# A four-layer sliding-attention kernel: a new set of planner costs and instruction orders, constant tables as planned tasks, weight scales computed in groups

## The chip, the core and the metric

The kernel runs on one core of a Trainium2 chip. A core has five engines that each work through their own instruction stream in order and wait for each other through semaphores: TensorE (PE, matmuls; its weight loads are listed as PEld), VectorE (DVE), ScalarE (ACT), GpSimd (POOL) and SyncE (SP, which here only starts DMA transfers). SBUF is the memory that the engines work in, PSUM the eight accumulator banks that PE writes and DVE and ACT read. The metric is the device time of one execution in microseconds, the median of several runs. All times below are in us unless marked ns.

## What is computed

Four layers A, B, A, B on `x` of 2048 positions by 512, each `x = x + layer(layernorm(x))`, with 32 heads of 16. Layer A is a dilated local attention: each position sees eight positions, 0, 2, ..., 14 back. Layer B is a block attention: each position sees itself and the 255 before it.

```
def _A_ref(x, wqkv, wo):            # W, dil = 8, 2
    q, k, v = split(x @ wqkv)
    idx = pos[:, None] - off[None, :]            # off = 0, 2, ..., 14
    logits = einsum("bhsd,bhswd->bhsw", q, k[idx]) * scale
    attn = softmax(where(idx >= 0, logits, -1e9))
    return einsum("bhsw,bhswd->bhsd", attn, v[idx]) @ wo

def _B_ref(x, wqkv, wo):            # W = 256
    q, k, v = split(x @ wqkv)
    scores = einsum("bhqd,bhkd->bhqk", q, k) * scale
    mask = (i - j >= 0) & (i - j < W)
    return einsum("bhqk,bhkd->bhqd", softmax(where(mask, scores, -1e9)), v) @ wo

x = x + A(layernorm(x));  x = x + B(layernorm(x))       # and both once more
```

## The kernel before

The sequence is cut into eight chunks of 256 positions. The work is done chunk by chunk in pairs of layers: `layer_a(0, c)` and `layer_b(1, c)` for c = 0 to 7, then `layer_a(2, c)` and `layer_b(3, c)`. In the tables these sixteen pairs are called A0, B0 to A15, B15. All matmuls of the projections are done with a high and a low half of both operands in 16 bits: `xh`, `xl` of the normalized input, `wA0h`, `wA0l` and so on of the weights (s = 0, 1, 2 for q, k, v and 3 for the output).

Before any projection the weights are prepared by `prep` (L765), for A and then for B. For each of the four parts: two DMA loads of 512 KB (into the buffers `stk`, which hold layer B's stacked operands later, or into `stage` for the output weights); the sum of squares per partition (L807 on ACT, L809 on DVE); two transposes on PE that put it in one row; on DVE a chain of a reduce and five operations on one number (L823 to L829, called a scale chain below); a matmul with ones that spreads the two factors to all partitions (L832); a copy to `psc` (L836); and then a split in two halves each, the high one on ACT (L860), the low one on DVE (L864). The first B loads use the `stk` buffers of A's weights and so wait for A's splits.

`norm` (L875) takes a chunk's statistics on DVE (L888 to L894), the power -0.5 on POOL (L897, operand `mhalf`), one more small operation on DVE (L900), normalizes on ACT (L915), transposes on PE (L919) and splits into `xh` (L924, ACT) and `xl` (L925, DVE). `proj_t` (L944 to L946) and `proj_n` (L964 to L967) are the projections.

`layer_a` (L1018) forms products of q with shifted k, four tiles `pr` per group and four groups (L1077, on DVE, some on POOL), which PE reduces over the head's 16 elements with the selector `sel` (L1085). Softmax follows (L1108 to L1120), its last operation a high/low split. PE spreads the weights over the head's elements with `selt` (L1154); DVE multiplies with v (L1167, the weighing, tiles `pw`, three buffers); the sum over the eight positions is three operations on POOL (L1174 to L1176) or one reduce on DVE (L1172). `finish` (L978) splits the result (L987, L989), projects it and adds it to x (L995).

`layer_b` (L1183) writes its q and k halves to DRAM and reads them back stacked (L1208, L1219). A first set of scores (L1262, L1265) only serves the row maximum: DVE overwrites the masked part (L1284) and reduces (L1280). In the first chunk of a layer there is nothing before it, and one custom operation does mask and maximum (L1276). The maximum goes to the operand by a DMA (L1317, L1323), and a second set of scores (L1356, L1358) goes through the exponential on ACT (L1362) and a mask on POOL (L1371) to the matmul with v (L1388). The sums come back through DRAM, and the division is a multiplication on DVE or POOL (L1462).

What sets the order: every piece above is a task, handed to `Plan.add` with its engine, a duration in us, what it reads and writes, and sometimes another engine (`alt`). The table `ORDER` holds one number for each task, its place in its engine's queue; a negative number -1 - n means place n on the other engine. `Plan.order` plays the tasks through with the durations, the `LAG` between engines, the cost `LEAVE` of a change in the kind of matmul, and DMA sizes; each engine takes its tasks in the order of places, and the play decides in which order the program is written out and which PSUM bank and buffer a task gets. On the chip every engine then follows its stream. The tables `maskt`, `sel`, `selt` and the ones in `v` are built on POOL before the first task. 330 matmuls without use (L1497, 110 tasks of three, table "W") keep PE active where it would idle.

## Time and profile before

| | |
|---|---|
| median of 3 runs | 1451.04 (1451.01 to 1454.21) |
| profiled execution | 1455.91 |
| its span, first to last instruction | 1454.0 |
| mean granted TensorE clock over the span | 0.969 |
| instructions | 35256 |
| DMA | 97.40 MB, mean 67 GB/s |

The profile is of one execution. Its own time is 4.9 above the median of the three runs, and 1.9 of it lies outside the span. A row of a timeline gives start, length, engine, line, operation, output and input, count, and in brackets the idle time of the engine before it with what ended it. A row by group gives the count, then busy time and mean ns of one, then idle time. In windows, busy time of each engine in each stretch is followed by the granted clock of TensorE, 1.00 being full speed.

### The profile page before, as it was taken

What the parts mean: (1) busy time and instruction counts of PE and PEld (TensorE: products, weight loads), DVE (VectorE), ACT (ScalarE), POOL (GpSimd) and SP (SyncE); (2) the same over time, 40 slices, a digit from 0 to 9 for tenths busy, and PEclk for the clock granted to TensorE, in tenths of its full rate; (3) what the DMA queues carried; (4) which work ended last, traced back from release to release, by engine and by line L of the source; (5) the groups of instructions that cost most, each with busy time, mean ns of one, the idle gap of its engine ahead of it and who ended that gap; (6) DMA issues with size and microseconds to landing.
All of it is one profiled execution on the core that took longest, in us unless ns stands there. A gap on an engine that the chain in (4) does not pass through costs nothing.

```text
span 1454.0 us, 35256 instructions
## 1 busy us (share of the span) xinstructions
PE 1351.0 (93%) x14058; PEld 796.1 (55%) x14058; DVE 1197.2 (82%) x2313; ACT 735.1 (51%) x1051; POOL 656.0 (45%) x752
## 2 busy tenths in 40 slices
PE   7698999989899999999989998998999999998998
PEld 4374655637465463745537364654647456474654
DVE  7958699797978979798887869798797988979693
ACT  6431335554555555555554434555454555545654
POOL 2504145372724627263471716446272553717342
PEclk9899899999999999999999998999999999999999
DMA  7030122212221221212122222222222122122221
GB/s 260 16 86 24 42 61 66 72 44 89 49 68 50 71 85 37 96 38 71 57 51 90 54 90 51 68 59 53 82 55 92 36 76 64 51 83 54 71 70 44
DMA packets 89221, 97.40 MB, mean 67 GB/s; under 512 B 34016, under 2 KB 60128, under 8 KB 89056
## 3 DMA queue, kind: packets, MB, share of 16 engines
q1 hardware_dynamic: 88800, 94.89, 23.2%
q8 instruction: 110, 1.80, 0.5%
q14 instruction: 55, 0.45, 0.1%
q10 hardware_dynamic: 256, 0.26, 0.1%
HBM read 50.33 MB, written 35.09 MB: 59 GB/s over the span
## 4 chain that ended last, share of the span: by engine, by line
PE 53%; DVE 22%; POOL 10%; issue 5%; DMA 5%; ACT 4%; SPq 1%; DVEq 0%; POOLq 0%; ACTq 0%
PE banks L944 9%; PE banks L945 8%; PE banks L946 8%; PE banks L1388 6%; DVE m L1280 4%; PE banks L1085 4%; POOL pw L1174 3%; DVE pw L1167 3%; DVE banks L1284 3%; PE banks L1356 3%; PE banks L966 3%; PE banks L964 2%; PE banks L1262 2%; PE banks L967 2%; PE banks L919 2%
## 5 line engine op out<-in xcount | busy, mean ns | idle before, releaser
L1362 ACT ACTIVATE p<-banks,sclB 128x768 f32<-128x768 f32 x480 | 419.8, 900 | 269.0 <-PE banks L1358 202.8
L1371 POOL TENSOR_SCALAR_AFFINE_SELECT p<-p 128x1024 f32<-128x1024 f32 x240 | 263.8, 1105 | 414.7 <-ACT p L1362 381.0
L1280 DVE TENSOR_REDUCE m<-banks 128x2 f32<-128x512 f32 x448 | 298.2, 685 | 5.0
L1284 DVE COPY_PREDICATED banks<-maskt,banks 128x256 f32<-128x256 int16 x448 | 180.6, 422 | 68.5 <-PE banks L1265 58.3
L1388 PE MATMUL banks<-p,v 128*32 128x128 f32 (+1 forms) x3840 | 197.0, 331 | 5.5 <-POOL p L1371 4.3
L1077 DVE TENSOR_TENSOR pr<-kv,q 128x512 f32<-128x512 f32 x239 | 162.9, 733 | 40.4 <-PE banks L1085 14.1
L1388 PEld LDWEIGHTS banks<-p,v 128*32 128x32 f32 x3840 | 106.0, 109 | 100.1 <-issue 38.0
L1167 DVE TENSOR_TENSOR pw<-banks,kv 128x1024 f32<-128x1024 f32 x128 | 152.6, 1213 | 2.9 <-POOL o L1176 2.0
L1356 PE MATMUL banks<-stk,stk 64*128 64x256 f16 x960 | 134.9, 282 | 21.5 <-DVE m L1280 6.6
L1174 POOL TENSOR_TENSOR pw<-pw 128x512 f32<-128x512 f32 x101 | 128.3, 1270 | 15.1 <-DVE pw L1167 14.5
L1262 PE MATMUL banks<-stk,stk 48*128 48x128 f16 (+1 forms) x896 | 112.8, 253 | 20.5 <-DVE m L1280 9.8
L1265 PE MATMUL banks<-stk,stk 48*128 48x256 f16 (+1 forms) x1024 | 127.1, 249 | 4.6 <-DVE pw L1167 1.9
L1356 PEld LDWEIGHTS <-stk 64*128 64x128 f16 x960 | 56.2, 95 | 104.7 <-issue 100.1
L1358 PE MATMUL banks<-stk,stk 64*128 64x128 f16 x960 | 108.0, 221 | 0.0
L1262 PEld LDWEIGHTS <-stk 48*128 48x128 f16 x896 | 50.3, 94 | 102.9 <-issue 98.7
L915 ACT ACTIVATE xn<-x,rs 128x512 f32<-128x512 f32 x64 | 52.0, 812 | 77.6 <-DVE rs L900 62.5
L1175 POOL TENSOR_TENSOR pw<-pw 128x256 f32<-128x256 f32 x101 | 74.8, 741 | 7.9
L1085 PE MATMUL banks<-pr,sel 128*32 128x512 f32 x512 | 70.4, 602 | 2.6 <-DVE pr L1077 2.5
L944 PE MATMUL banks<-xh,wB1h 128*128 128x256 f16 x256 | 70.6, 276 | 0.0
L944 PE MATMUL banks<-xh,wA2h 128*128 128x256 f16 x256 | 70.4, 275 | 0.1
L945 PE MATMUL banks<-xl,wA0h 128*128 128x256 f16 x256 | 69.8, 273 | 0.7 <-DVE xl L925 0.7
L944 PE MATMUL banks<-xh,wB0h 128*128 128x256 f16 x256 | 70.0, 274 | 0.4 <-DVE el L1198 0.4
(184 smaller groups left out, 3049.3 us busy)
## 6 DMA issues: line engine op xcount, KB each, us to landing
stk<-re SPq DMA_DIRECT2D x256, 96.0 KB
re<-eh SPq DMA_DIRECT2D x128, 128.0 KB
re<-el SPq DMA_DIRECT2D x64, 128.0 KB
oc<-os SPq DMA_DIRECT2D x120, 64.0 KB
os<-scr SPq DMA_DIRECT2D x15, 512.0 KB
x<-in_A_x_dram SPq DMA_DIRECT2D x8, 512.0 KB
xd<-x SPq DMA_DIRECT2D x16, 256.0 KB
x<-xd SPq DMA_DIRECT2D x8, 512.0 KB
```

Of the source, the lines that this page charges most:

```text
L944: nc.tensor.matmul(ps[mp].t[:, i], wh, xh, start=k == 0, stop=False)
L945: nc.tensor.matmul(ps[mp].t[:, i], wh, xl, start=False, stop=False)
L1077: E.tensor_mul(pr.t, window(kv[1].t, m, 64 * tq, 64)[:, 0], qb)
L1167: nc.vector.tensor_mul(pw.t, pb.t.unsqueeze(1).broadcast_to([P, 2, W, 64]), v)
L1174: E.tensor_add(t[:, :, 0:4], t[:, :, 0:4], t[:, :, 4:8])
L1262: nc.tensor.matmul(ps.t[:, par, 0 : (2 - qb) * P], lhs, stk[hf, bef][r, col, qb * P :], start=True, stop=True)
L1280: nc.vector.tensor_reduce(out=m.t[:, :, u, qb], in_=ps.t[:, :, 0 : 2 * P], op=ALU.max, axis=AX.X)
L1284: nc.vector.copy_predicated(t[:, :, 0:P], maskt[:, 0:P].bitcast(I16).unsqueeze(1).broadcast_to([P, 2, P]), t[:, :, 2 * P : 3 * P])
L1356: nc.tensor.matmul(o[:, two], k[:, jf * P : (jf + 1) * P], q, start=True, stop=True)
L1362: nc.scalar.activation(pt.t[:, :, 2 * i : 2 * i + 2].rearrange("p s m q -> p m s q"), ps.t[:, :, : 3 * P].rearrange("p m (s q) -> p m s q" ...
L1371: nc.gpsimd.affine_select(out=v, in_=v, pattern=[[0, 8], [-1 if b == 0 else 1, P]], compare_op=ALU.is_gt if b == 0 else ALU.is_ge, fill=0. ...
L1388: nc.tensor.matmul(o, v[:, jj, 17 * h : 17 * h + 32], rhs, start=z == 0 and (b == 0 or first), stop=z == 1 and b == 1, tile_position=(0, 3 ...
```

## The change

The planner's costs, the orders and four pieces of the program change; what is computed stays.

1. Every row of `ORDER` is replaced. One row before and after stands for all:

```
-    "A0": [0, 1, 3, 0, 2, 4, 3, 5, 1, 10, 5, 11, 4, 14, 9, 15, 0, 2, 22, 23, 24, 25, 26, 27, 28, 30, 39, 41, 45, 46,
+    "S": [3, 1, 6, 5],
+    "A0": [0, 0, 2, 1, 3, 4, 4, 5, 2, 19, 5, 13, 4, 28, 8, 18, 0, 2, 41, 42, 43, 44, 45, 46, 47, 53, 59, 60, 64, 65,
```

2. Durations and latencies of the planner, and the time from which each engine is free:

```
+SCALES = {"A": ((0,), (1,), (2, 3)), "B": ((0, 1, 2, 3),)}
+FROM = {"PE": 1.6, "DVE": 0.8, "ACT": 2.1, "POOL": 1.6, "SP": 0.8}
-LAG = {"PE": 0.23, "DVE": 0.13, "ACT": 0.16, "POOL": 0.1, "SP": 0.0}
+LAG = {"PE": 0.24, "DVE": 0.13, "ACT": 0.16, "POOL": 0.1, "SP": 0.0}
-LEAVE = {"C": 0.185, "H": 0.19, "R": 0.13, "F": 0.105, "": 0.0}
+LEAVE = {"C": 0.12, "H": 0.04, "R": 0.1, "F": 0.1, "": 0.0}
-        plan.add("DVE", 0.98, bottom, r=[vt1], w=[vrx])
-        plan.add("DVE", 0.47, over, r=[vrx, vmx], w=[vov])
+        plan.add("DVE", 1.07, bottom, r=[vt1], w=[vrx])
+        plan.add("DVE", 0.57, over, r=[vrx, vmx], w=[vov])
-                    plan.add("DVE", 0.28 + 2 * (3 * P - x0) / 960 if first else 0.61, top, r=[vps], w=[v])
+                    plan.add("DVE", 0.41 + 2 * (3 * P - x0) / 960 if first else 0.61, top, r=[vps, vmask], w=[v])
-            plan.add("SP", 1.25, mget, r=[vmd], w=[vst[hf, "m", hp]], size=4)
+            plan.add("SP", 0.55, mget, r=[vmd], w=[vst[hf, "m", hp]], size=4)
...
```

3. The constant tables become four tasks on POOL that are placed by the row "S", and their readers wait for them:

```
+    plan.begin("S")
+    for us, f, v in ((0.6, set_ones, vones), (1.5, set_mask, vmask), (0.9, set_sel, vsel), (3.0, set_selt, vselt)):
+        plan.add("POOL", us, f, w=[v])
...
-            plan.add("PE", 0.5, spread, r=[veh, vel], w=vpb, mode="H", act=0.213)
+            plan.add("PE", 0.5, spread, r=[veh, vel, vselt], w=vpb, mode="H", act=0.213)
```

4. `prep` makes the scales of a group at once. A group of n parts has one reduce of the 2n sums per partition (`most`), one transpose, one scale chain on n partitions, and, for n above 1, one more operation that puts the factors on a diagonal so that one matmul with ones spreads them all:

```
+            def most(am=am, ax=ax, n=n):
+                nc.vector.tensor_reduce(out=ax.t[:, 0:n], in_=am.t[:, 0:n], op=ALU.max, axis=AX.X)
+
+            plan.add("DVE", 0.12, most, r=vam, w=[vax])
+            plan.add("PE", 0.3, lambda pt=pt, ax=ax, n=n: nc.tensor.transpose(pt.t[0:n, 0:P], ax.t[:, 0:n], idf), r=[vax], w=[vpt])
...
+                if n > 1:
+                    nc.vector.tensor_tensor(out=b[:, 0:n], in0=b[:, n : n + 1].broadcast_to([n, n, 2]),
+                                            in1=idf[0:n, 0:n].unsqueeze(2).broadcast_to([n, n, 2]), op=ALU.mult)
...
+            plan.add("DVE", 1.0 if n == 1 else 1.2, one, r=[vpt], w=[va])
+            plan.add("PE", 0.3, spreads, r=[va], w=[vpb])
```

A's parts 0 and 1 keep a chain of their own, its parts 2 and 3 share one, and B's four share one: four scale chains in place of eight, 4 small transposes and 4 spreading matmuls in place of 16 and 8.

5. The matmuls without use read `idf`, the identity, seen as 16-bit numbers, in place of `selt`; there are as many as before. The low split of a weight may go to POOL, which the new orders use nowhere.

Between the engines the new table moves 17 more of the products `pr` from DVE to POOL (34 of 256 there, 17 before) and 4 more of the multiplications L1462 (16 of 30, 12 before); one sum over eight positions goes from POOL to DVE (28 of 128 on DVE, 27 before). In the changed file the lines behind `prep` are numbered 43 higher.

The order changes everywhere; three places show how. First POOL at the start of the program, before (`rs` at L897 is the power in the first chunk's norm, `pad` a block of zeros for layer B's operands):

```order
L738 MEMSET sel 128x128
L740 AFFINE_SELECT sel<-sel 128x128
L742 AFFINE_SELECT sel<-sel 128x128
L747 MEMSET selt 128x256
L750 AFFINE_SELECT selt<-selt 32x256 x4
L1046 MEMSET kv_0_1_189 128x4x14
L1477 MEMSET pad_193 16x256
L1479 MEMSET pad_193 2x256
L1046 MEMSET kv_0_2_200 128x4x14
L897 TENSOR_TENSOR rs_0_244<-rs_0_244,mhalf 128x2
```

and now, in the same place on POOL:

```order
L734 MEMSET v_125 128x2x16
L735 MEMSET v_125 128x2x32
L940 TENSOR_TENSOR rs_0_223<-rs_0_223,mhalf 128x2
L753 MEMSET selt 128x256
L756 AFFINE_SELECT selt<-selt 32x256 x4
L745 MEMSET sel 128x128
L747 AFFINE_SELECT sel<-sel 128x128
L749 AFFINE_SELECT sel<-sel 128x128
L1520 MEMSET pad_302 16x256
L1522 MEMSET pad_302 2x256
```

The power now stands ahead of `selt`, `sel` and the pads, behind the mask and the ones. Second, DVE where the first chunk of layer A ends and layer B's first norm begins, before (`wB1l` and `wB3l` are low splits, `x` the update by L995):

```order
L1172 TENSOR_REDUCE o_0_702<-pw_0_3_1_765 128x2x64
L843 TENSOR_SCALAR sclB_185<-pscB_178,pscB_181 128x1
L995 SCALAR_TENSOR_TENSOR x_0_191<-banks,sclA_171,x_0_191 128x512
L989 TENSOR_TENSOR ol_0_763<-o_0_702,oh_0_757 128x4x128
L888 BN_STATS b_0_817<-x_0_191 128x6
L864 SCALAR_TENSOR_TENSOR wB1l<-stk_1_118,pscB_175,wB1h 128x512 x2
L864 SCALAR_TENSOR_TENSOR wB1l<-stk_1_121,pscB_175,wB1h 128x512 x2
L995 SCALAR_TENSOR_TENSOR x_0_191<-banks,sclA_171,x_0_191 128x512
L888 BN_STATS b_0_817<-x_0_191 128x6
L891 BN_AGGR mv_0_855<-b_0_817 128x2 x2
L894 TENSOR_SCALAR rs_0_858<-mv_0_855 128x2
L900 SCALAR_TENSOR_TENSOR rs_0_858<-mv_0_855,rs_0_858 128x2
```

and now:

```order
L1032 TENSOR_TENSOR ol_0_760<-o_0_718,oh_0_753 128x4x128
L902 SCALAR_TENSOR_TENSOR wB0l<-stk_0_120,pscB_142,wB0h 128x512 x2
L1038 SCALAR_TENSOR_TENSOR x_0_153<-banks,sclA_141,x_0_153 128x512
L931 BN_STATS b_0_800<-x_0_153 128x6
L1038 SCALAR_TENSOR_TENSOR x_0_153<-banks,sclA_141,x_0_153 128x512
L934 BN_AGGR mv_0_804<-b_0_800 128x2
L931 BN_STATS b_0_800<-x_0_153 128x6
L934 BN_AGGR mv_0_804<-b_0_800 128x2
L937 TENSOR_SCALAR rs_0_808<-mv_0_804 128x2
L943 SCALAR_TENSOR_TENSOR rs_0_808<-mv_0_804,rs_0_808 128x2
L902 SCALAR_TENSOR_TENSOR wB0l<-stk_0_117,pscB_142,wB0h 128x512 x2
L902 SCALAR_TENSOR_TENSOR wB1l<-stk_1_118,pscB_142,wB1h 128x512 x2
```

The four half splits of `wB1` went from between the two updates of x to behind the norm, with a pair of `wB0`; the other pair of `wB0` stands ahead of the updates. Third, POOL in the fourth chunk of the second layer A (A11), where products were moved most; before:

```order
L897 TENSOR_TENSOR rs_3_11798<-rs_3_11798,mhalf 128x2
L1371 AFFINE_SELECT p_1_3_1_11838<-p_1_3_1_11838 128x1024
L1371 AFFINE_SELECT p_1_3_0_11698<-p_1_3_0_11698 128x1024
L1065 COPY ha_3_1_12041<-kv_3_1_11135 128x56
L1371 AFFINE_SELECT p_1_4_0_12006<-p_1_4_0_12006 128x1024
L1371 AFFINE_SELECT p_1_4_1_12072<-p_1_4_1_12072 128x1024
L1048 COPY kv_4_1_12232<-ha_3_1_12041 128x4x14
```

and now:

```order
L940 TENSOR_TENSOR rs_3_11753<-rs_3_11753,mhalf 128x2
L1414 AFFINE_SELECT p_1_3_1_11724<-p_1_3_1_11724 128x1024
L1120 TENSOR_TENSOR pr_3_0_0_11930<-kv_3_1_11108,q_3_11905 128x512
L1120 TENSOR_TENSOR pr_3_0_1_11948<-kv_3_1_11108,q_3_11905 128x512
L1414 AFFINE_SELECT p_1_3_0_11783<-p_1_3_0_11783 128x1024
L1108 COPY ha_3_1_11999<-kv_3_1_11108 128x56
L1120 TENSOR_TENSOR pr_3_1_0_12011<-kv_3_1_11108,q_3_11905 128x512
L1120 TENSOR_TENSOR pr_3_1_3_12030<-kv_3_1_11108,q_3_11905 128x512
L1120 TENSOR_TENSOR pr_3_1_2_12048<-kv_3_1_11108,q_3_11905 128x512
L1414 AFFINE_SELECT p_1_4_0_11960<-p_1_4_0_11960 128x1024
```

Five of the chunk's sixteen products, all on DVE before, stand on POOL between the masks of the layer B chunk that runs at the same time (L1371, now L1414).

248 lines of the change are left out of this document (138 added, 110 removed), and 820 rows, old and new, of the table ORDER.

## The prediction

> **What bounds the kernel now.** I read the page first: how busy each engine is over the span and what clock TensorE was granted.
>
> ```profile
> PE 1351.0 (93%) x14058; PEld 796.1 (55%) x14058; DVE 1197.2 (82%) x2313; ACT 735.1 (51%) x1051; POOL 656.0 (45%) x752
> PEclk9899899999999999999999998999999999999999
> ```
>
> TensorE (PE) is busy for 93% of the span, VectorE (DVE) for 82%: PE is the bound on average, DVE is second. The average hides stages, so I cut the span where its character changes. The columns are the stretch, its length, each engine's busy time and count, then the granted clock.
>
> ```profile
> core 0: us, PE busy (x) PEld busy (x) DVE busy (x) ACT busy (x) POOL busy (x), PEclk, DMA share, GB/s
> 57.00:86.00 29.00, 18.24 (x90) 10.73 (x91) 26.73 (x41) 9.47 (x12) 15.89 (x20) 0.71 0.09 14
> 100.00:170.00 70.00, 62.90 (x457) 34.71 (x456) 52.68 (x159) 18.77 (x31) 21.67 (x28) 0.90 0.12 35
> 170.00:815.00 645.00, 615.15 (x6590) 361.37 (x6587) 545.41 (x999) 333.38 (x475) 302.80 (x339) 0.98 0.23 65
> 815.00:915.00 100.00, 91.20 (x806) 48.85 (x803) 81.84 (x204) 43.31 (x66) 54.20 (x64) 0.93 0.25 66
> 915.00:1440.00 525.00, 499.48 (x5644) 296.05 (x5642) 439.47 (x798) 286.85 (x403) 245.66 (x264) 0.99 0.23 64
> ```
>
> Two things stand here. Until 86 us PE has little to do: in 57 to 86 DVE is busy 26.73 of 29, and PE issues 90 matmuls; this is the head, one chunk of layer A with nothing to overlap it. After 100 us PE is the bound, with a rest: idle time of 7.1 + 29.9 + 8.8 + 25.5 = 71.3 us, and a granted clock below 1, which costs 0.10 x 70 + 0.02 x 645 + 0.07 x 100 + 0.01 x 525 = 32 us by the rounded clocks. So about 103 of the 1340 us are what a better order could still fetch there. Two short stretches show how gap and clock belong together.
>
> ```profile
> 640.00:655.20 15.20, 13.22 (x147) 5.52 (x145) 15.20 (x23) 8.56 (x13) 14.49 (x17) 1.00 0.23 48
> 655.20:658.70 3.50, 3.50 (x27) 0.97 (x25) 3.50 (x6) 1.75 (x3) 3.41 (x5) 0.51 0.41 94
> ```
>
> From 640 to 655 DVE is busy without a break and POOL almost so, PE loses 2.0 us in small gaps, and right behind them the clock is at half for 3.5 us, which costs another 1.7. A gap is thus paid nearly twice. DVE is the local bound there, though PE is the bound on average.
>
> **The head, in four stretches.** The chain of waits shows where the head's time goes (start, length, what):
>
> ```profile
> 53.74 1.29 POOL pw L1174
> ...
> 71.48 0.46 POOL o L1176
> 73.91 2.73 DVE wB1l L864 x4
> ```
>
> and these are the rows at its start, on POOL and then on DVE:
>
> ```profile
> 8.36 0.71 POOL L897 TENSOR_TENSOR rs<-rs,mhalf 128x2 f32<-128x2 f32 x1
> 24.83 1.66 POOL L897 TENSOR_TENSOR rs<-rs,mhalf 128x2 f32<-128x2 f32 x1 [15.76 <-DVE rs L894]
> ```
>
> ```profile
> 6.16 0.59 DVE L894 TENSOR_SCALAR rs<-mv 128x2 f32<-128x2 f32 x1
> 9.10 0.16 DVE L900 SCALAR_TENSOR_TENSOR rs<-mv,rs 128x2 f32<-128x2 f32 x1 [2.35 <-POOL rs L897]
> ```
>
> with the anchors on DVE that bound the stretches:
>
> ```profile
> 26.60 2.49 DVE L1077 TENSOR_TENSOR pr<-kv,q 128x512 f32<-128x512 f32 x4
> ...
> 52.45 2.35 DVE L1167 TENSOR_TENSOR pw<-banks,kv 128x1024 f32<-128x1024 f32 x2
> ...
> 82.97 1.41 DVE L925 TENSOR_TENSOR xl<-banks,xh 128x512 f16<-128x512 f32 x2
> ```
>
> and the prices, by group (mean ns of one behind the bar's busy time):
>
> ```profile
> L823 DVE TENSOR_REDUCE a1A<-banks 1x1 f32<-1x256 f32 x4 | 1.6, 406 | 1.4 <-PE banks L817 1.4
> L824 DVE TENSOR_SCALAR a1A<-a1A 1x1 f32<-1x1 f32 x4 | 0.6, 142 | 0.1
> L864 DVE SCALAR_TENSOR_TENSOR wA2l<-stk,pscA,wA2h 128x1024 f16<-128x1024 f32 x2 | 2.6, 1278 | 0.0
> L809 DVE CUSTOM_DVE_ANT_0 wA0l<-stk 128x1024 bf16<-128x1024 f32 x1 | 1.2, 1219 | 0.0
> L1167 DVE TENSOR_TENSOR pw<-banks,kv 128x1024 f32<-128x1024 f32 x128 | 152.6, 1213 | 2.9 <-POOL o L1176 2.0
> L1172 DVE TENSOR_REDUCE o<-pw 128x128 f32<-128x1024 f32 x27 | 51.9, 1924 | 0.0
> L1174 POOL TENSOR_TENSOR pw<-pw 128x512 f32<-128x512 f32 x101 | 128.3, 1270 | 15.1 <-DVE pw L1167 14.5
> L1175 POOL TENSOR_TENSOR pw<-pw 128x256 f32<-128x256 f32 x101 | 74.8, 741 | 7.9
> L1176 POOL TENSOR_TENSOR o<-pw 128x128 f32<-128x128 f32 x101 | 46.4, 459 | 7.9
> ```
>
> One scale chain on DVE (a reduce and five small operations) is 0.41 + 5 x 0.14 = 1.1 us.
>
> Start to the first products (26.60): the power on POOL could begin when L894 ends, at 6.75, and began at 8.36, because the constant tables stood ahead of it; now `selt`, `sel` and the pads stand behind: 1.6 us. They cost nothing there: POOL's next row after the 8.36 one begins at 24.83, so it has room. DVE does two scale chains instead of three (1.1) and four splits instead of five (1.28), with two squares as before. Together 4.0, but projections, their copies on ACT and the weights' landing must keep up; I take 2.5, bounds 1 and 4.
>
> Products to the first weighing (52.45): three scale chains become two with one small operation more each (0.8 less); the rest of the exponentials moves from POOL (1.15) to DVE (about 0.7); one split pair of B goes too (2.3). Against that two more splits of A and one square of B come in (2 x 1.28 + 1.22 = 3.8), and two of the splits stand ahead of the fourth group of products. About nothing; bounds -2 and +1.
>
> Weighing to the last sum of the chunk (71.94): six of the eight sums were on POOL, 1.27 + 0.74 + 0.46 = 2.47 us each, with one 1.1 us subtraction: 18.2 us from 53.74. Now five are on POOL and three on DVE: POOL needs 5 x 2.47 + 1.15 = 13.5, DVE 8 x 1.21 + 3 x 1.92 = 15.5, and with the waits for the three buffers the stretch is set by DVE at about 15.5 from the first weighing, where it took 19.5: 4.0, bounds 2 and 4.5. The two scale chains and the two splits that stood among the weighings are gone from there.
>
> Last sum to the first operand of layer B (84.3): the four half splits of `wB1` (2.73) between the two updates of x go behind the norm, one pair of `wB0` (1.9) comes in their place; but behind the norm 1.9 + 2.7 now stand ahead of L925, where three splits of `wB2` and `wB3` stood under ACT's and PE's work. About -0.5, bounds -3 and +1.
>
> Head: 2.5 + 0 + 4.0 - 0.5 = **6 us**, bounds -2 and 10. PE is the bound from there on, so I carry it to the end whole. Grouping B's four scales makes its splits wait for the last weight, but all stand after the weighing anyway, so its cover is the chunk's own work; without it the wait would be the last load's.
>
> **The two stages with a chunk 0 of layer B** (100 to 170, 815 to 915). They lose 15.9 us idle and 14 us of clock in 170, 18%, while the other 1170 us lose 73, 6%. At 6% they would lose 11: 19 us are to be had. What is special there is the masked maximum on DVE, L1276, which the old planner priced at 0.55 and 0.81 us for its two sizes, 0.68 on average.
>
> ```profile
> L1276 DVE CUSTOM_DVE_ANT_0 j<-banks,maskt 128x256 bf16<-128x256 f32 (+1 forms) x128 | 45.4, 355 | 21.6 <-PE banks L1265 9.8 <-PE banks L1085 0.2 <-PE banks L1388 0.2
> L1276 DVE DVE_READ_ACCUMULATOR2_ANT m<- 128x1 f32 x128 | 10.5, 82 | 0.0
> L1114 DVE TENSOR_REDUCE mx<-e 128x64 f32<-128x512 f32 x16 | 16.6, 1039 | 1.0 <-ACT e L1137 0.8
> L1117 DVE RECIPROCAL mx<-mx 128x64 f32<-128x64 f32 x16 | 8.8, 553 | 0.5
> ```
>
> A task is two pairs of them, 2 x (0.355 + 0.082) = 0.87 us, so 64 tasks were planned 12 us too short; the new price averages 0.81 and closes two thirds. A good price only allows a good order, so I take less than two thirds of 19: **8 us**, bounds 0 and 19.
>
> **The other stages.** The sum L1114 (planned 0.98, now 1.07, row 1.04) and the reciprocal L1117 (0.47, now 0.57, row 0.55) were short by 0.14 a chunk, 2 us over 14. The order itself moves 17 products and 4 multiplications from DVE to POOL and one sum back: 17 x 0.68 + 4 x 0.82 - 1.9 = 13 us off DVE, the engine that is full where the gaps are. PE switches between kinds of matmul as often as before, and its work is the same but for 16 tiny matmuls, so only gaps and clock can give. The upper bound is the 15 us of DVE, the lower 0, since the sampled stretch is full of weighings, which do not move. I take the middle, **8 us**.
>
> [...]
>
> **The sum.** The profiled execution took 1455.9 (span 1454.0 and 1.9 around it); 6 + 8 + 8 = 22 leave 1433.9. The median of the three runs is 1451.0, 4.9 below the profiled one, so **1429**.
>
> **The rivals.** (A) Only the head is gained and the rest comes out as before: 1451 - 6 = 1445. For it: the weighing stretches stay as full as they are. (B) The order, planned with the chip's own durations, closes two fifths of all 103 us: 1451 - 6 - 41 = 1404. For it: nearly all of it sits in many small gaps, each paid twice. Against it: PE's switches and the sharing of DVE and ACT work are the same. (C) The change does not do what it says: the head's gain is given back in the next stage, and 1451 stays.
>
> (D) Slower, by one mechanism: the 21 moved operations read two tensors from SBUF, and while POOL runs such a one DVE cannot.
>
> ```profile
> 182.42 1.09 DVE L1309 SCALAR_TENSOR_TENSOR mt<-mr,mt 128x32 f16<-128x32 f32 x1 [0.30 <-ACT mt L1304]
> ```
>
> ```profile
> 182.28 1.18 POOL L1077 TENSOR_TENSOR pr<-kv,q 128x512 f32<-128x512 f32 x1
> ```
>
> ```profile
> L1077 DVE TENSOR_TENSOR pr<-kv,q x239: 643/684/1679, 26.6 to 1308.6; 128x512 f32<-128x512 f32 x120
> L1077 POOL TENSOR_TENSOR pr<-kv,q x17: 1177/1187/1734, 182.3 to 1210.2; 128x512 f32<-128x512 f32 x17
> ```
>
> The small L1309 took 1.09 us beside a product on POOL and ended with it, and products on DVE reach 1679 ns where the median is 684: about 0.9 us of DVE's time a time. Behind it on DVE stand products that the matmul L1085 waits for. If two thirds of the 21 reach PE, that is 14 x 0.9 and, with four more half-clock stretches at 1.7, some 7 more: 1451 - 6 + 19 = 1464. It decides from about seven of them on, if the stages give nothing. [...]
>
> **How the numbers follow.** Forecast 0.39, A 0.17, B 0.24, C 0.06, D 0.14. From no change this kernel can be told at 0.3%, 4.4 us: the forecast and B are faster, A is 0.11 faster and 0.06 the same, C is 0.04 the same and 0.01 each way; D is slower but for 0.01. Faster 0.75, same 0.11, slower 0.14. The likeliest has 1415 to 1443 as its own range (head -2 to 10, stages 0 to 19 and 0 to 15, not all at one end). The range reaches down to B's time with some 6 below, 1398, and up to most of D, 1458; what is outside is a deep B and the rest of D.
>
> **What would show it.** Right: POOL's first power (L897 before) starts before 7.5 us; the last sum of the first chunk ends near 66; layer B's first L925 comes near 78; PE's idle time in the two chunk-0 stages falls below 12 us and their clock to 0.95 or more. Wrong: DVE still busy 26 of 29 us up to 86; products on DVE with a mean over 0.8 us and PE waiting for L1077 more than now (D); PE's idle after 100 us at 71 or more (A).

## The result, and the profile after

| | before | after |
|---|---|---|
| median (four runs of each, beside each other) | 1452.62 (1451.01 to 1454.39) | 1465.20 (1463.98 to 1466.46) |
| profiled execution | 1455.91 | 1465.40 |
| its span | 1454.0 | 1463.7 |
| mean granted clock | 0.969 | 0.956 |

The change makes the kernel slower by 12.6: the ratio is 1.0086, interval 1.0068 to 1.0105. The prediction had the wrong sign, and its range, up to 1458, does not hold the time. The two profiled executions are only 9.5 apart, since that of the kernel before is 3.3 above its median; what the traces below account for is this 9.5.

The page of the changed kernel, busy time and clock:

```profile
PE 1357.8 (93%) x14038; PEld 791.5 (54%) x14038; DVE 1183.3 (81%) x2270; ACT 735.7 (50%) x1052; POOL 677.8 (46%) x770
PEclk9799999999999999999999998999999999999999
```

The five stretches of the prediction, now cut out of the changed kernel (same columns):

```profile
57.00:86.00 29.00, 16.94 (x86) 9.88 (x87) 25.80 (x34) 14.16 (x20) 11.46 (x15) 0.70 0.03 3
100.00:170.00 70.00, 61.89 (x465) 36.21 (x464) 52.00 (x163) 18.21 (x28) 22.78 (x29) 0.90 0.15 41
170.00:815.00 645.00, 614.67 (x6531) 356.59 (x6530) 538.79 (x978) 334.75 (x481) 317.03 (x350) 0.97 0.24 64
815.00:915.00 100.00, 90.21 (x816) 49.19 (x815) 81.11 (x204) 42.72 (x63) 53.48 (x62) 0.91 0.24 63
915.00:1440.00 525.00, 499.60 (x5562) 286.86 (x5564) 430.38 (x782) 286.43 (x402) 254.72 (x274) 0.98 0.23 63
```

DVE is 14 us less busy over the span than before and POOL 22 more, as the change says. But PE idles 8.1 + 30.3 + 9.8 + 25.4 = 73.6 us, where it idled 71.3, and its clock is lower in three of the four stretches; by the rounded clocks it costs 7 + 19 + 9 + 11 = 46 us, where it cost 32. None of the 103 us that a better order could fetch was fetched: they became nearly 120.

The waits of PE from 100 to 1440, summed by what ended them (as far as the semaphores tell), show where the idle time went. Those for DVE fall from 40.4 to 35.8, as the change intended; those for ACT rise from 21.1 to 25.2 and those for transfers from 0.5 to 5.4.

The head did become shorter. POOL's powers (the first operation of each norm that waits for the chunk before), in the changed kernel and then in the kernel before:

```profile
6.56 0.71 POOL L940 TENSOR_TENSOR rs<-rs,mhalf 128x2 f32<-128x2 f32 x1 [2.82 <-DVE rs L937]
...
73.97 0.70 POOL L940 TENSOR_TENSOR rs<-rs,mhalf 128x2 f32<-128x2 f32 x1 [7.08 <-DVE rs L937]
149.00 0.70 POOL L940 TENSOR_TENSOR rs<-rs,mhalf 128x2 f32<-128x2 f32 x1 [3.33 <-DVE rs L937]
```

```profile
78.50 0.70 POOL L897 TENSOR_TENSOR rs<-rs,mhalf 128x2 f32<-128x2 f32 x1 [6.40 <-DVE rs L894]
154.69 0.70 POOL L897 TENSOR_TENSOR rs<-rs,mhalf 128x2 f32<-128x2 f32 x1 [4.17 <-DVE rs L894]
```

Layer B's first norm is 4.5 us earlier, the next one 5.7. From there the lead is lost piece by piece: at the norms up to 577 it lies between 2 and 5 us, it is gone at 666, and from 1270 on the changed kernel is late: 6 us there, 8 near 1356, 9.7 at the end. No single place loses it.

What is lost can be counted. In the trace, PE's lost time behind 100 us, up to its last matmul, is its idle time plus half of its busy time at half clock (there a matmul of 256 columns starts 0.213 us behind the one before it, at the median of both traces, and at full clock 0.109):

| | last matmul ends | idle | half clock: us, stretches | its cost | idle + cost |
|---|---|---|---|---|---|
| before | 1450.3 | 73.3 | 71.7, 12 | 32.0 | 105.3 |
| after | 1459.1 | 76.9 | 102.4, 15 | 45.6 | 122.5 |

So the change loses 13.6 us at half clock and 3.6 to idle time, and gains 4.5 in the head; the last matmul ends 8.8 later, so some 4 more must be gained in work or in short waits that the profile shows as busy.

### The profile page after: what moved, and what is told of

Same layout as the page of the kernel before. It is cut to its first block, busy times and chain, and to the rows that moved or that the text cites. A ratio compares the mean times of both kernels' runs of the same rounds, so it can differ in the third digit from the quotient of the medians.

```text
span 1463.7 us, 35148 instructions
## 1 busy us (share of the span) xinstructions
PE 1357.8 (93%) x14038; PEld 791.5 (54%) x14038; DVE 1183.3 (81%) x2270; ACT 735.7 (50%) x1052; POOL 677.8 (46%) x770
## 4 chain that ended last, share of the span: by engine, by line
PE 54%; DVE 19%; DMA 8%; POOL 6%; issue 5%; SPq 4%; ACT 4%; DVEq 0%; ACTq 0%; POOLq 0%
PE banks L987 8%; PE banks L988 7%; PE banks L989 7%; PE banks L1431 6%; PE banks L1009 4%; PE banks L1399 4%; PE banks L1007 4%; PE banks L1128 4%; DVE m L1323 3%; PE banks L1010 3%; DVE pw L1210 3%; DVE banks L1327 3%; PE banks L1305 3%; POOL pw L1217 2%; PE banks L1308 2%
## 5 line engine op out<-in xcount | busy, mean ns | idle before, releaser
L1414 POOL TENSOR_SCALAR_AFFINE_SELECT p<-p 128x1024 f32<-128x1024 f32 x240 | 261.1, 1094 | 403.4 <-ACT p L1405 382.6
L1120 DVE TENSOR_TENSOR pr<-kv,q 128x512 f32<-128x512 f32 x222 | 153.0, 744 | 35.2 <-PE banks L1128 15.9
L1308 PE MATMUL banks<-stk,stk 48*128 48x128 f16 (+1 forms) x1024 | 127.3, 252 | 8.4 <-DVE m L1319 3.7
L1305 PE MATMUL banks<-stk,stk 48*128 48x128 f16 (+1 forms) x896 | 112.3, 253 | 22.4 <-DVE m L1323 6.8
L1241 DVE SCALAR_TENSOR_TENSOR el<-banks,eh 128x512 f16<-128x512 f32 x64 | 43.1, 684 | 46.9 <-ACT eh L1238 25.6
L1120 POOL TENSOR_TENSOR pr<-kv,q 128x512 f32<-128x512 f32 x34 | 44.5, 1319 | 71.7 <-PE banks L1128 30.3
L987 PE MATMUL banks<-xh,wA0h 128*128 128x256 f16 x256 | 70.0, 274 | 2.4 <-DVE xl L968 1.3
```

The lines of the kernel that those rows point to most:

```text
L987: nc.tensor.matmul(ps[mp].t[:, i], wh, xh, start=k == 0, stop=False)
L1120: E.tensor_mul(pr.t, window(kv[1].t, m, 64 * tq, 64)[:, 0], qb)
L1305: nc.tensor.matmul(ps.t[:, par, 0 : (2 - qb) * P], lhs, stk[hf, bef][r, col, qb * P :], start=True, stop=True)
L1308: nc.tensor.matmul(ps.t[:, par, (2 - qb) * P : 3 * P], lhs, stk[hf, now][r, col, : (1 + qb) * P], start=True, stop=True)
L1414: nc.gpsimd.affine_select(out=v, in_=v, pattern=[[0, 8], [-1 if b == 0 else 1, P]], compare_op=ALU.is_gt if b == 0 else ALU.is_ge, fill=0. ...
```

## The experiments

Four theories were set against each other, and the expectations call them so: T1, the new order leaves PE too little work in some places, and the clock drops to half behind them; T2, DVE sets the pace in those places and the clock is a symptom; T3, the operations moved to POOL, or the transfers, hold DVE and PE up; T4, the planner's new prices (PE's in the first place) are further from the chip than the old ones. Ratios are to the kernel before on the same chip, which ran 17 to 23 times beside each group.

### The head alone

`h_head` has the change's program, tables as tasks, grouped scales and its order up to 104 us of the plan; behind it stand the old prices and, for every task, the old order and the old sharing between engines.

```
-LAG = {"PE": 0.24, "DVE": 0.13, "ACT": 0.16, "POOL": 0.1, "SP": 0.0}
+LAG = {"PE": 0.23, "DVE": 0.13, "ACT": 0.16, "POOL": 0.1, "SP": 0.0}
-LEAVE = {"C": 0.12, "H": 0.04, "R": 0.1, "F": 0.1, "": 0.0}
+LEAVE = {"C": 0.185, "H": 0.19, "R": 0.13, "F": 0.105, "": 0.0}
...
-                dma = max(dma, t.end + 0.65) + t.size / 390.0
-                landed = dma + 0.65
+                dma = max(dma, t.end + 0.9) + t.size / 390.0
+                landed = dma + 0.9
...
```

> The changed program with the new order for everything that was planned to start in the first 104 us and for the whole preparation of the weights, and behind that every engine's order and sharing as before, planned with the old costs. If the new order behind 104 us is what loses: the head's 4.5 us are kept and the time is 1444 to 1450. If the head itself leaves a state that costs later (its erosion began at 150 us): 1455 or more.

Measured: 1452.71, ratio 0.999 (0.9975 to 1.0005). Its powers on POOL:

```profile
74.03 0.70 POOL L936 TENSOR_TENSOR rs<-rs,mhalf 128x2 f32<-128x2 f32 x1 [7.12 <-DVE rs L933]
...
154.19 0.70 POOL L936 TENSOR_TENSOR rs<-rs,mhalf 128x2 f32<-128x2 f32 x1 [3.14 <-DVE rs L933]
```

The same 4.5 us are there at 74, and 0.5 is left at 154, under the old order: the stage behind the head was not waiting for all of it. Some of the lead comes back; at most of the later norms `h_head` is about 2 us ahead of the kernel before. The time lies in neither of the two ranges expected, and by its interval the head is worth at most 3.6 us and perhaps nothing. So the loss of 12.6 us comes from prices, order and sharing behind the head.

### Filling the thin places

In both traces the clock changes on a grid of 3.41 us: the 29 changes before and the 35 after all stand on it, to within 3 ns. To see what stands ahead of a fall, I count a matmul's columns at full clock (0.107 us for 256, where the median step from one matmul of 256 to the next is 0.109 in both traces) and weight them with the share of the 128 rows that it uses. Most falls behind 100 us follow a slot of 3.41 us with 1.25 us of such work or less: 11 of 12 before and 11 of 15 after, leaving out one in each kernel that comes behind the last matmul. The other five stand at 1.6 to 1.9, and the thinnest slots without a fall have 1.3. Idle time separates worse: slots ahead of a fall have 0.8 to 2.5 us of it, others up to 1.6. In 17 of these 27 slots DVE is busy for 95% or more, and in 20 of them it does a weighing. One such place, cut out of the changed kernel and then of the kernel before:

```profile
1247.70:1252.00 4.30, 2.79 (x39) 1.30 (x33) 4.30 (x8) 2.53 (x5) 3.79 (x6) 1.00 0.27 91
1252.00:1258.80 6.80, 6.47 (x33) 1.75 (x29) 5.37 (x6) 4.59 (x6) 6.49 (x9) 0.50 0.27 45
```

```profile
1247.00:1252.00 5.00, 4.31 (x36) 1.69 (x36) 5.00 (x8) 2.69 (x4) 4.69 (x7) 1.00 0.24 36
1252.00:1258.80 6.80, 5.48 (x56) 2.38 (x51) 6.51 (x13) 3.94 (x6) 6.27 (x7) 1.00 0.40 98
```

DVE is full in both until 1252; PE is busy 65% of the stretch after the change and 86% before, and only the first is followed by 6.8 us at clock 0.50.

To test T1, `a_fill` (after) and `b_fill` (before) put matmuls without use into such places, two ahead of a chosen task into its own fresh bank; `a_ctrl` puts about as many ahead of tasks elsewhere; `a_lean` and `b_lean` take fewer places. They add work only.

```
+FILL = {"B0": (99, 101, 114, 116, 120, 127, ...), "A1": (117, 124), ...}
...
+            if t.k in FILL.get(t.scope, ()):
+                v = idf.bitcast(F16)
+                for _ in range(EXTRA):
+                    nc.tensor.matmul(psum[:, fresh[0].at, 0 : 2 * P], v[:, 0:P], v, start=True, stop=True)
```

> The changed kernel with 298 more matmuls without use (two of 256 columns each, 0.107 us at full clock) ahead of 149 PE tasks, written into the bank that the task fills next, placed where a stretch of 3.41 us of its trace streams less than 1.3 us worth of columns: the ends of the weighings. Orders, banks and buffers stay. Theory 1 (the added time is half-clock time, set off by thin PE work there): half-clock time behind 100 us falls from 104 us to below 40, and the time from 1465 to between 1440 and 1458, although PE gets 32 us more work. Theory 2 (DVE sets the pace of those stretches and the clock is only a symptom): half-clock time falls as well, but the time stays within 3 us of 1465 or rises. Theory 3 (POOL's products block DVE, or waits for DMA): no effect on either, 1465 to 1490 by the added matmuls.

> The kernel before with the same kind of filling, 254 matmuls ahead of 127 PE tasks, chosen from its own trace by the same rule. Theory 1: its half-clock time behind 100 us falls from 72 us to below 30 and the time from 1452 to between 1436 and 1450; the distance between the two filled kernels shrinks from 12.6 us to below 6. Theory 2: no gain, 1452 to 1475. Theory 3: 1452 to 1475, and the distance to the changed kernel stays near 12.

> Control: the changed kernel with 250 of the same matmuls ahead of 125 tasks some 35 us behind each thin stretch, where PE has enough to do. Theory 1: half-clock time stays near 104 us and the time rises by 10 to 27 us (up to 0.107 us each, less what falls into idle time), 1475 to 1492. If the time falls here too, the place of the filling does not matter and theory 1 is wrong.

> The changed kernel with the thinner filling by the same rule, 175 matmuls (18.7 us) ahead of 92 tasks; its extra time at half clock is 38.0 us. Theory 1: 1450 to 1460, below the 1465 of the changed kernel, and nearer to the thinly filled kernel before than 12.6 us by the 5 to 10 us that the clock cost more here. Theory 2: 1466 to 1484.

> The kernel before with a thinner filling: 129 matmuls without use (13.8 us at full clock) ahead of 68 tasks, no more than bring every 3.41 us of its own trace to 1.3 us of streamed columns, at tasks with idle time of PE behind them. By task and kind, PE work behind 90 us takes 27.6 us longer at half clock than the same kinds take at full clock. If that time is really lost on the path (theory 1, now with its price): about half of it comes back and most of the filling falls into idle time, 1440 to 1449, faster than both kernels. If DVE sets the pace there (theory 2): 1453 to 1467.

| | matmuls added (us at full clock) | median | ratio | half clock from 100 to the end of the span |
|---|---|---|---|---|
| `a_fill` | 298 (31.9) | 1468.15 | 1.0112 (1.0095 to 1.0130) | 47.8 |
| `a_ctrl` | 250 (26.8) | 1489.93 | 1.0257 (1.0234 to 1.0279) | 95.2 |
| `a_lean` | 175 (18.7) | 1459.93 | 1.0056 (1.0034 to 1.0077) | 43.9 |
| `b_fill` | 254 (27.2) | 1456.45 | 1.0027 (1.0015 to 1.0038) | 33.6 |
| `b_lean` | 129 (13.8) | 1453.08 | 1.0019 (1.0004 to 1.0034) | 24.9 |

The change itself has a ratio of 1.0086 and, counted the same way, 104.5 us at half clock; the kernel before has 73.9. By the ratios, 32 us of useless work in the thin places cost the changed kernel 4 us, while 27 us elsewhere cost 25. The 19 us of `a_lean` gain 4, but its interval, 1.0034 to 1.0077, overlaps that of the change, 1.0068 to 1.0105. The spans and clocks of `a_fill` and then of `a_ctrl`:

```profile
core 0: 1470.5 us, clock 0.974
```

```profile
core 0: 1488.2 us, clock 0.958
```

Half the time at half clock goes, and that pays for the filling. So the place of the filling matters, as T1 says, and `a_ctrl` came out in its range. That it is nearly free fits T2 as well, since PE had gaps there: `a_fill`, `b_fill` and `b_lean` came out at times that T2 expected and not T1, and only `a_lean` reached the upper edge of T1's range. If its gain is real, the clock is a cause and not only a symptom; the runs do not settle it. And the clock alone does not carry the loss: with more than half of the half-clock time gone from both, the two kernels are still 11.7 apart, with the leaner filling 6.9, and the kernel before gains nothing by either. Part of that may be the filling itself, of which the changed kernel has 5 us more in both cases.

The kernel before shows the same size in its own scatter: its 105 runs among the experiments, on five chips, lie between 1446.5 and 1460.9 at clocks of 0.963 to 0.976, 0.75 us of time per 0.001 of clock (correlation -0.75). The change's clock is 0.013 lower, some 10 us by that slope, which is most of the 12.6. This is a correlation, not a test, and the fillings, which raised the clock without winning that time, speak for less.

### Products on POOL

`b_pool` is the kernel before with 18 products and 4 multiplications moved from DVE to POOL and all else in its order; `a_unpool` is the changed kernel with 19 products and 2 multiplications back on DVE. In the table of places that is a sign:

```
-    "B2": [..., 527, ...],
+    "B2": [..., -136, ...],
```

> The kernel before with one part of the change alone: 18 products and 4 multiplications that the change has on POOL go there from DVE, at the moment that was planned for them; all else keeps its order. About 15 us of work leave DVE. If DVE's load is what the later stages wait for (the prediction's third term): 1444 to 1449. If POOL's two-input operations hold DVE up (rival D): 12 of them reach PE at 0.9 us each with two or three more half-clock stretches, 1463 to 1469. If neither matters because PE is the bound and its order is what counts: 1450 to 1457.

> The changed kernel with 19 products and 2 multiplications taken back from POOL to DVE, all else in its order. Third term of the prediction: slower, 1470 to 1475. Rival D: 1450 to 1456. Neither: 1462 to 1468.

Measured: `b_pool` 1460.79, ratio 1.0064 (1.0043 to 1.0085); `a_unpool` 1465.16, ratio 1.0090 (1.0068 to 1.0112). The products by group on DVE and POOL, in the kernel before, in `b_pool` and in the changed kernel:

```profile
L1077 DVE TENSOR_TENSOR pr<-kv,q 128x512 f32<-128x512 f32 x239 | 162.9, 733 | 40.4 <-PE banks L1085 14.1 <-ACT kv L1058 13.0 <-ACT q L1056 12.7
L1077 POOL TENSOR_TENSOR pr<-kv,q 128x512 f32<-128x512 f32 x17 | 23.5, 1387 | 37.4 <-PE banks L1085 17.3 <-ACT kv L1058 14.9 <-ACT q L1056 5.2
```

```profile
L1073 DVE TENSOR_TENSOR pr<-kv,q 128x512 f32<-128x512 f32 x221 | 162.2, 784 | 41.5 <-PE banks L1081 15.3 <-ACT kv L1054 13.0 <-ACT q L1052 12.6
L1073 POOL TENSOR_TENSOR pr<-kv,q 128x512 f32<-128x512 f32 x35 | 49.9, 1439 | 58.0 <-PE banks L1081 22.5 <-ACT q L1052 20.5 <-ACT kv L1054 14.9
```

```profile
L1120 DVE TENSOR_TENSOR pr<-kv,q 128x512 f32<-128x512 f32 x222 | 153.0, 744 | 35.2 <-PE banks L1128 15.9 <-ACT kv L1101 13.3 <-ACT q L1099 5.5
L1120 POOL TENSOR_TENSOR pr<-kv,q 128x512 f32<-128x512 f32 x34 | 44.5, 1319 | 71.7 <-PE banks L1128 30.3 <-ACT kv L1101 28.8 <-ACT p L1405 6.3
```

Before, 239 products took DVE 162.9 us at 733 ns (the prediction's list has the median, 684). With 18 fewer, `b_pool` needs 162.2 at 784 ns: the moved ones leave, and those that stay take as much longer. DVE's whole busy time goes from 1197.2 to 1196.7, POOL's from 656.0 to 687.3. So moving 22 operations of together some 15 us freed half a microsecond, and cost 0.6% of the time. The change's own order places them better: DVE is busy 1183.3, and 1187.9 in `a_unpool`, 4.6 us for 21 operations. In `a_unpool` the 241 products on DVE take 718 ns at the mean, 744 in the change. But the time is the same with and without them, as expected if neither DVE's load nor rival D decides. The products do get longer, as rival D has it. In the trace before, 15 of DVE's products begin while POOL runs one: 14 of them end 0.55 to 0.65 us behind POOL's and take up to 1.68, where the 220 that overlap no product on POOL have a median of 0.684; the other one began with POOL's, took 0.68, and POOL's took 1.73. Not all of DVE is held: 13 of the row maxima L1280 overlap a product on POOL and keep their 0.68 to 0.69 us. In `b_pool` the longer products and the moves cost 9.3 us, half of the 19 written for D and less than the range expected. It isn't what makes the change slow.

### Prices and searches

If the order behind the head is at fault, is it because its prices are wrong? First `a_oldcosts`: the change's orders, played with the old prices. Only banks, buffers and the order of writing out differ from the changed kernel.

> The changed program and its orders, but played through with the old costs, so that only the banks and buffers that tasks get and the order in which the program is written out differ. By the old prices its planned end is 1505, and three kernels planned with them took 26 us more on the chip than planned (1425.8 and 1452, 1427.0 and 1452.7, 1434.0 and 1460.8). If an order only fits the prices under which it was found: well over 1475, up to 1531. If banks and buffers do not matter: 1462 to 1468.

Measured: 1500.45, ratio 1.0310 (1.0286 to 1.0335); its plan ended at 1505. The same orders lose another 35 us when other prices choose their banks, their buffers and the order of writing out. So an order can't be judged apart from the prices that it is played with.

So new orders were searched for. Each search starts from the change's orders, moves one task at a time to another place or to its other engine, plays the plan, and keeps what ends earlier. `s_new` uses the change's prices; `s_cal` mends those of PE, which T4 blames; `s_leave` has only `LEAVE` back at its old values; `s_dma` has only the transfers' latency back; `s_old` starts from `h_head` with all the old prices. `s_cal2`, `s_new2`, `s_dma2` and `s_dma3` repeat a search with other random numbers. The edit of prices in `s_cal` and then in `s_dma`, beside the rows of `ORDER`:

```
-LEAVE = {"C": 0.12, "H": 0.04, "R": 0.1, "F": 0.1, "": 0.0}
+LEAVE = {"C": 0.12, "H": 0.065, "R": 0.064, "F": 0.1, "": 0.0}
...
-                    plan.add("PE", 0.172, scores, r=[vst[hf, 0, hp], vst[hf, now, hp], *([] if first else [vst[hf, bef, hp]])],
+                    plan.add("PE", 0.211, scores, r=[vst[hf, 0, hp], vst[hf, now, hp], *([] if first else [vst[hf, bef, hp]])],
...
```

```
-                dma = max(dma, t.end + 0.65) + t.size / 390.0
-                landed = dma + 0.65
+                dma = max(dma, t.end + 0.9) + t.size / 390.0
+                landed = dma + 0.9
```

> Theory 4: the change's own price table is what went wrong. By the traces, PE's work behind 90 us takes 1257 us at full clock; the old table plans 1260 for it, the new one 1224, because it lowers the cost of leaving a kind of matmul (rightly) but leaves a scores task (two pairs of matmuls, 992 of them) at 0.172, where it takes 0.211 if the next one is of its kind. This kernel is the changed program with that price at 0.211 and the leaving costs as measured, and with orders found from the new ones by 2.3 million small trial moves; its planned end falls from 1451.7 to 1427.1. If the price of PE led the search astray: 1438 to 1452, at least 13 us faster than the changed kernel. If prices do not matter and the loss is elsewhere: 1460 to 1468.

> Control for it: the same start and as many trial moves, with the change's own prices; the planned end falls from 1417.3 to 1412.1. Theory 4: no gain, 1460 to 1468, since the plan is improved in a currency that the chip does not pay in. If any further search helps: 1455 to 1460.

> The kernel with the new head and the order of before behind it (1452.7), searched on for as many trial moves with the old prices, whose sum for PE is right; planned end from 1427.0 to 1420.2. Theory 4: the chip follows by most of it, 1444 to 1449, faster than both kernels. If plan and chip have nothing to do with each other at this scale: 1451 to 1458.

> The same with only the costs of leaving a kind of matmul put back to those of before (0.185, 0.19, 0.13, 0.105), a scores task at 0.172 as in the change. The sum planned for PE is then near 1257 again; the changed orders plan 1475.3 and the search brings that to 1426.9. Theory 4: what counts is that the sum is right, wherever it sits: 1443 to 1452. If it was the price of the scores task itself: 1456 to 1466.

> A search from the changed orders with another price altered: a transfer's latency back from 0.65 to the 0.9 of before, PE's prices as in the change. With it the changed orders plan 1465.4, and 2.7 million trial moves bring that to 1416.6. Theory 4 (PE's price): the plan is still too light in PE, so 1456 to 1466. If any altered price and a new search do it: 1444 to 1453, as with PE's price mended.

> The search with the mended price of PE once more with other random moves; planned 1428.5. Theory 4: within 4 us of the first (1444 to 1452). If the first was luck: 1455 to 1465.

> The search with the change's own prices once more with other random moves; planned 1410.9, lower than all others. Theory 4: 1457 to 1467. If a lower plan means a faster kernel whatever the prices: below 1448.

> A second search from the change's orders with only the transfers' latency back at 0.9, other random numbers than in the first (which measured 1441.96; this one's plan ends at 1420.1, that one's at 1416.6). If that price is what matters: 1438 to 1448, PE idle behind 100 us under 68 and waits for DMA under 4 us, as in the first. If every searched order is a draw around the same time, whatever the price: anywhere in 1445 to 1463, and 1455 is as likely as 1447.

> The same search a third time (plan 1420.2). If the latency's price matters: within 6 us of the first two, all three below 1448. If each order is a draw: the three spread over 8 us or more, as 1448.1 and 1462.6 did with PE's price mended and 1463.1 and 1454.1 with the change's own prices; one of the two new ones then lies above 1450.

| | latency | plan ends | median | ratio | PE's waits for DMA | idle, cost of half clock |
|---|---|---|---|---|---|---|
| before | 0.9 | 1425.8 | | 1 | 0.5 | 73.3, 32.0 |
| after | 0.65 | 1417.3 | 1465.20 | 1.0086 (1.0068 to 1.0105) | 5.4 | 76.9, 45.6 |
| `s_new` | 0.65 | 1412.1 | 1463.13 | 1.0058 (1.0037 to 1.0079) | 11.4 | 78.7, 34.5 |
| `s_new2` | 0.65 | 1410.9 | 1454.12 | 1.0008 (0.9991 to 1.0026) | 9.2 | 71.0, 39.3 |
| `s_cal` | 0.65 | 1427.1 | 1448.10 | 0.9959 (0.9944 to 0.9974) | 7.0 | 68.3, 27.2 |
| `s_cal2` | 0.65 | 1428.5 | 1462.64 | 1.0062 (1.0038 to 1.0086) | 9.6 | 76.6, 30.0 |
| `s_leave` | 0.65 | 1426.9 | 1452.09 | 0.9990 (0.9972 to 1.0008) | 6.1 | 73.1, 24.1 |
| `s_old` | 0.9 | 1420.2 | 1450.38 | 0.9964 (0.9949 to 0.9978) | 1.8 | 71.9, 31.5 |
| `s_dma` | 0.9 | 1416.6 | 1441.96 | 0.9915 (0.9899 to 0.9931) | 2.7 | 63.6, 27.7 |
| `s_dma2` | 0.9 | 1420.1 | 1448.63 | 0.9960 (0.9945 to 0.9975) | 2.8 | 66.4, 32.5 |
| `s_dma3` | 0.9 | 1420.2 | 1443.46 | 0.9933 (0.9915 to 0.9951) | 2.3 | 63.3, 30.6 |

Three things follow.

The plan's end says little. `s_new2`, with the earliest end of all, is 12 us slower than `s_dma`. Two searches with the same prices differ by 14.5 us (`s_cal`, `s_cal2`) and 9.0 (`s_new`, `s_new2`), the three of `s_dma` by 6.7. The first `s_cal` alone, in the range that T4 expected, seemed to prove T4 for PE's price; its repeat is 14.5 us slower, and the two pairs overlap, so PE's price can't be told from the scatter. Of the other expectations, `s_new` and `s_cal2` fell into one of their ranges and `s_leave` to the edge of one; `s_old` and `s_new2` lie between theirs, and `s_dma` is faster than both of its own. `s_dma2` missed the range for the latency by 0.6 us and lies in the wide one for chance. The three of `s_dma` spread by 6.7 us, which is less than the 8 or more expected of chance, but they are not all below 1448 as expected of the latency.

One price separates the groups. The four new orders found at a latency of 0.9 have ratios of 0.9915 to 0.9964, the five found at 0.65 have 0.9959 to 1.0062, and the change, the sixth at 0.65, 1.0086. One order at 0.65, `s_cal`, lies among the fast ones. Where the latency is the only price that differs, the groups are clear of each other: 0.9915, 0.9933 and 0.9960 against 1.0008, 1.0058 and the change. The waits suggest how. PE's waits for a transfer behind 100 us, in the changed kernel and then in `s_dma`:

```profile
PE banks L1308 <- DMA stk<-re: 2.7, 3, 1.8
...
PE banks L1305 <- DMA stk<-re: 1.7, 2, 1.1
...
PE banks L1399 <- DMA stk<-md: 1.0, 1, 1.0
```

```profile
PE banks L1395 <- DMA stk<-md: 1.0, 2, 0.5
...
PE banks L1304 <- DMA stk<-re: 0.9, 1, 0.9
PE banks L1301 <- DMA stk<-re: 0.8, 2, 0.5
```

PE's own waits are 5.4 to 11.4 us in every order found at 0.65 and at most 2.8 in every new one at 0.9; over all engines these waits are 60 to 84 us against 37 to 47. In the changed kernel's trace the stacked operands land 2.57 us after their issue, at the median, and 3.3 us from the first of a task's two issues; 95% of the tasks take 3.1 or more. The plan has 1.23 + 0.65 + 0.49 + 0.65 = 3.0 us there, less than nearly all of them, and with 0.9 it would have 3.5, a margin of 0.2 over the median.

That this margin is what makes these orders faster is not shown by itself. The kernel before was planned at 0.9 too, has the smallest of these waits (0.5) and is slower than the four new orders; beside it `s_dma` gains in PE's waits for DVE, 30.4 us where the kernel before has 40.4. And a rival stands untested: `s_new` and `s_new2` start from orders that already fit their prices (1417.3 planned, 1412.1 and 1410.9 found), while the new price throws `s_dma` back to 1465.4, from where it searches far. Against that rival stand `s_cal2` and `s_leave`, which were thrown back as well: the one is slower than the kernel before, the other the same. `s_cal`, thrown back too, is faster.

The best order beats both kernels: `s_dma` is 11.6 us faster than the kernel before in its own group. Its stretches:

```profile
57.00:86.00 29.00, 20.92 (x107) 12.98 (x108) 22.26 (x30) 15.43 (x21) 7.09 (x9) 0.70 0.06 7
...
100.00:170.00 70.00, 63.99 (x502) 37.30 (x495) 53.36 (x168) 20.35 (x32) 22.40 (x28) 0.95 0.16 42
170.00:815.00 645.00, 618.13 (x6609) 356.62 (x6608) 550.88 (x1027) 340.03 (x490) 320.20 (x361) 0.98 0.24 65
815.00:915.00 100.00, 93.26 (x889) 54.39 (x888) 82.98 (x188) 43.49 (x66) 42.31 (x48) 0.97 0.23 66
915.00:1440.00 525.00, 497.32 (x5480) 284.81 (x5478) 419.29 (x762) 278.52 (x392) 247.12 (x269) 0.98 0.24 64
```

Part of its gain stands where the prediction looked for it: in the two chunk-0 stages PE idles 6.0 + 6.7 = 12.7 us where it idled 15.9 before, at clocks of 0.95 and 0.97, and DVE is no longer full up to 86 us. That is 3.2 of the 9.7 us of idle time that it saves.

## Why the prediction was wrong

**Start to the last sum of the first chunk: right in mechanism, smaller than forecast.** The first power starts at 6.56, below 7.5. The anchors of the prediction in the changed kernel, with the first chunk's last sum:

```profile
24.75 2.50 DVE L1120 TENSOR_TENSOR pr<-kv,q 128x512 f32<-128x512 f32 x4 [0.81 <-ACT kv L1101]
...
51.55 2.34 DVE L1210 TENSOR_TENSOR pw<-banks,kv 128x1024 f32<-128x1024 f32 x2
...
66.03 1.90 DVE L1215 TENSOR_REDUCE o<-pw 128x128 f32<-128x1024 f32 x1
...
79.68 1.29 DVE L968 TENSOR_TENSOR xl<-banks,xh 128x512 f16<-128x512 f32 x2 [0.70 <-ACT xh L967]
```

The first products come 1.85 us earlier (2.5 forecast), the weighing 0.9 (2.5), since the stretch between grew by 0.95 instead of 0, and the last sum ends at 67.9 (near 66 forecast), 4.0 earlier (6.5). Layer B's first low split stands at 79.68, not 78: 3.3 of the 6 us.

**"PE is the bound from there on, so I carry it to the end whole": failed.** `h_head` has the 4.5 us at 74 and 0.5 at 154. Up to 170 PE is not yet the bound. PE's waits in `h_head` from 100 to 170 (total, times, longest):

```profile
PE banks L1304 <- DMA stk<-re: 1.7, 2, 1.2
PE banks L1395 <- DVE pw L1206: 1.6, 1, 1.6
PE banks L1304 <- DVE m L1315: 1.3, 4, 0.6
PE banks L1124 <- DVE pr L1116: 1.1, 1, 1.1
```

It idles 9.6 us there (7.1 before): 6.4 for DVE's products, weighings and masked maxima of the same stage (5.9 before), which a shorter head does not shorten, and 1.7 for transfers (none before). The step should have been priced in that stage, at nothing to 2 us.

**"A good price only allows a good order": the caution was right, the two terms of 8 us were not.** These terms carry 16 of the 22 us forecast. The masked maximum was repriced as worked out, but the chunk-0 stages idle 17.9 us (15.9 before; below 12 forecast), at clocks of 0.90 and 0.91 (0.95 or more forecast). Both terms rest on one step, that a plan nearer the chip gives an order that is faster on the chip. The change's plan ends 8.5 us earlier than that of the kernel before (1417.3 for 1425.8, each by its own prices) and its time is 12.6 later, and the runs show a scatter of 7 to 15 us between orders of the same prices and nearly the same planned end. The terms should have been 0 with a range of about 10 us to either side. Besides, one new price of the same table, the latency of 0.65, was never weighed in the prediction, and it goes with the slower group.

**"13 us off DVE": mis-sized.** The count of operations was right, the gain was not: they free 0.5 us in the order before and 4.6 in the new one, since DVE's remaining products get longer. DVE's busy time does fall by 13.9 in all, but 9.3 of that are there without these moves, in `a_unpool`. A sign of it was in the profile before: DVE's products have a mean of 733 ns beside their median of 684, with only 17 on POOL.

**"A gap is thus paid nearly twice": right, and it worked against the forecast.** The falls behind 100 us come behind slots of 3.41 us in which PE is idle for 0.8 to 2.5 us in all, and thin work marks them better than idle time does. The new order made three stretches more of them, 30.7 us at half clock, which cost 13.6 us.

**The rivals.** A and C expected no loss behind the head, and B that the order's prices pay; none came. C's mechanism, the head's gain given back in the next stage, is what `h_head` shows at 154, where 0.5 of 4.5 us is left; it does not account for the loss. D had the sign and nearly the time, 1464, but by luck: `b_pool` shows its mechanism at 0.6%, and `a_unpool`, with 21 of the operations back on DVE, is as slow as the change. Of the marks against, PE's idle time of 71 or more came true (73.6), and DVE's load up to 86 (25.8 of 29 us) nearly so; the products' mean stayed under 0.8 us, and PE waited for none of them behind 100 us (0.8 before).

**What stays open.** Shown is that the loss is behind the head, in prices, order and sharing, that it appears as half-clock time and a little idle time, and that POOL's products do not explain it. PE's prices could not be told from the scatter. Whether the half clock is the cause of the loss or follows from waits elsewhere is not settled. That the latency's price matters is supported by the three orders that differ in it alone, and its mechanism is argued. Why the change's order lies even above the other five at its latency was not found; by the scatter of repeated searches it may be a poor draw.

## What to carry to other kernels

When a planner's table is re-searched, the plan's end is no forecast: run several orders from different random numbers and keep the one that measures best, since here they scatter by 7 to 15 us, as much as any repricing was worth. A price above the median for transfers that the bound engine waits for is worth a try; here the three orders that differed in it alone were all faster, though the reason isn't shown. A gain at the start counts only if the stage behind it is shown to wait for it.

## What the runs showed of the hardware

- The granted clock moved in slots of 3.41 us, whose grid stood differently in the span of the two executions (first edge at 3.31 us in the profile before, 2.68 after); behind 100 us falls lasted one to three slots, in both traces. The kernel before varied by 7.5 to 11.8 us on one chip (17 to 23 runs on each of five), 0.75 us longer per 0.001 of clock less.
- PE was busy for part of each slot ahead of a fall, in both traces: 22 of the 27 falls behind 100 us followed slots with 1.25 us of work or less, counted at full clock, the other five slots with 1.6 to 1.9 us of it and 1.0 to 1.7 us of idle time.
- DVE's products lengthened from 733 to 784 ns at the mean when 18 of 239 went to POOL (`b_pool` against the kernel before), and POOL's own from 1387 to 1439: both sides paid.
